# U transposed on TensorE and normalised by VectorE from PSUM, with a longer ring of exp blocks

## The chip, the cores and the metric

The kernel runs on one core of one Trainium2 chip. The metric is the device time of one execution in microseconds. TensorE (PE) multiplies matrices into PSUM, ScalarE (ACT) and VectorE (DVE) read PSUM and write SBUF, GpSimd (POOL) works from SBUF to SBUF, and SyncE (SP) issues the DMAs. The five work from instruction lists of their own and meet by semaphores.

## The reference

A layer norm of x (2048 tokens of 640) feeds two branches whose results are added to x: attention with 32 query heads of 20 columns and one shared key and value head, and a dense pair of matrices with SiLU between.

```python
x = A_x
xn = _layernorm(x, axis=-1)
return x + _A_ref(xn, A_wq, A_wk, A_wv, A_wo) + _B_ref(xn, B_w1, B_w2)
# _A_ref: q = (x @ wq) as 32 heads of 20; k = x @ wk; v = x @ wv  (20 columns each)
scores = jnp.einsum("bhqd,bkd->bhqk", q, k) * (Dh ** -0.5)
p = _softmax(scores, axis=-1)
o = jnp.einsum("bhqk,bkd->bhqd", p, v)        # heads side by side, then @ wo
# _B_ref: silu(x @ w1) @ w2, w1 640x1728, w2 1728x640
```

## The kernel before

**Units, groups and steps.** A unit is one head for one chunk of 512 queries: 32 heads by 4 chunks make 128 units. Three units form a group (43 groups, the last with two). A group runs over 16 key tiles of 128; each of these 688 steps is one score tile S (`do_S`, matmuls at L747): three matmuls, one a unit, into three PSUM banks. Banks 0 to 2 and 3 to 5 take turns, so S of step t+2 needs the banks of step t read out.

**Exponentials on two engines.** In most steps ScalarE exponentiates two of the three banks in one instruction (exp, L765) into blocks of the ring `E`, and VectorE does the third: p1 (L779) clamps the score, scaled and shifted so that its int16 bits are a bfloat16 power of two, into `Z`; once three such blocks have come together, two instructions (y, L838) make two phase-shifted copies in `Y`, and the three versions are later summed with weights built into copies of v, which evens out the error of the bit trick. Where VectorE has too much queued (`want_dve`), in the first ten steps, and in the last step of a group, ScalarE takes all three banks. E has NBLK = 31 blocks of 512 columns; an exp whose blocks don't fit before the ring's end starts again at block 0 and waits until that has been read.

**PV.** For each step and each of the Y sets, TensorE multiplies v with the blocks (L826) into PSUM bank 6 (`UBANK`), four column strips of 32 rows at once: U, 21 rows a unit, of which the last is the softmax's sum. These matmuls trail the score tiles by some steps; `pv_q` holds the ones to come, and the ring E is their store.

**End of a group** (`end_group`, `norm_dma`). VectorE copies U to SBUF (L937), and bank 6 is free for the next group. SP transposes the copy by DMA (L896), GpSimd adds up the strips in four instructions (L904, L907, L909), VectorE takes the reciprocal of the sums (L914), and GpSimd multiplies into `o` (L923). The last group alone uses another way, on TensorE and VectorE (L949, L962, L978).

**Other TensorE work,** called misc, fills the time between: q of the next chunk (L1015), h = x @ w1 (L1049; tanh on ScalarE L1057, product on VectorE L1062), and output jobs (`out_job`: 14 matmuls with w2 at L1111, 5 with wo at L1116, evicted at L1128 and L1134), all through PSUM bank 7. Each job has a step before which it may not start. What is left of it after the last S runs alone: for the last chunk's output these are eight jobs of 14 matmuls each and the short ones with wo. Matmuls of zeros (fills, L671 and L684) keep TensorE busy in gaps.

**Order.** It is made at build time by a list scheduler (`Sched`, `Builder.step`) with assumed durations. TensorE takes S when it may start, else PV or misc, not starting one that would run more than OVER past the time at which S is due. VectorE and ScalarE take the ready instruction of lowest priority number: U evacuation and reciprocal 0.9 (U_PRIO), p1 1.0, q, h and output evictions 1.6 (X_PRIO), y 4.0. `lock` keeps y and the GpSimd instructions of `norm_dma` from being planned at the same time; on the chip nothing enforces that. SP keeps plain loads in order but may pass them with q copies and transposes.

**Prologue.** x is loaded, normalised, transposed; k, v and the first q tiles are made, among them a dense q tile; the scaling of wo by 2 on GpSimd follows the k tiles. Score tiles start within the prologue; PV may start when the prologue's jobs are done or 11 PVs wait (PV_HOLD).

Of the kernel before, what the change touches and what calls it, by code (L numbers as in the profile page):

```python
# [7 lines left out]
BF16 = mybir.dt.bfloat16  # L8
F32 = mybir.dt.float32
# [5 lines left out]
P = 128  # L15
# [29 lines left out]
NUNITS = H * QC  # L45
NBLK = 31
NZ = 3
# [16 lines left out]
DT_ISSUE = 1.28  # L64
UT_ISSUE = 1.05
DT = (4, 5, 6, 7, 11, 12, 13, 14, 15)
# [9 lines left out]
class Op:  # L76
    __slots__ = ("eng", "dur", "fn", "deps", "prio", "seq", "end", "avail", "idx", "inc", "inc_no", "sem",
                 "on_sched", "name", "dma", "mode", "start", "mm", "work", "kt", "na", "rs", "re", "rl", "then", "after", "lock")

    def __init__(self, eng, dur, fn, deps, prio=0.0, name="", on_sched=None, mode=None):  # L80
        self.eng = eng
        self.dur = dur
        self.fn = fn
        self.deps = deps
        self.prio = prio
        self.name = name
        self.on_sched = on_sched
        self.mode = mode
        self.start = None
        self.end = None  # L90
# [9 lines left out]
        self.lock = False  # L100

# [5 lines left out]
class Sched:  # L107
    def __init__(self, nc, stack):
# [11 lines left out]
        self.held = {}  # L120
        self.lock_end = {"dve": 0.0, "pool": 0.0}
        self.busy = defaultdict(float)
# [42 lines left out]
    def ready(self, op, extra=0.0):  # L165
        r = 0.0
        for d in op.deps:
# [9 lines left out]
            if a > r:  # L177
                r = a
        if op.lock:
            r = max(r, self.lock_end["pool" if op.eng == "dve" else "dve"])  # L180
        return r

    def commit(self, op, start):
# [3 lines left out]
        if op.dma:  # L187
            if op.name in ("oTd", "xTd", "uTd"):
                self.dma_t = op.end
            self.dma_t = max(getattr(self, "dma_t", 0.0), op.end) + op.mode / 230e3  # L190
            op.avail = op.end + 1.6 if op.name in ("oTd", "xTd", "uTd") else max(op.end + 2.0, self.dma_t + 1.6)
        else:
            op.avail = op.end + LAT[e]
# [3 lines left out]
        self.busy[e] += op.dur  # L197
        if op.lock:
            self.lock_end[e] = op.end
        self.held[e] = op.then  # L200
# [3 lines left out]
    def run(self):  # L204
        wake = {e: 0.0 for e in self.engs}
        while True:
# [13 lines left out]
            else:  # L220
# [122 lines left out]
class Builder:  # L343
# [17 lines left out]
    def alloc(self):  # L361
# [185 lines left out]
    def step(self, now):  # L547
# [64 lines left out]
        if choice == "PV":  # L612
# [115 lines left out]
    def do_S(self, t, now):  # L728
# [78 lines left out]
        pv.kt = kt  # L807
        self.pv_last = pv
        pv.na = na
# [19 lines left out]
    def flush_z(self):  # L829
# [7 lines left out]
        for k in range(2):  # L837
            sc.new("dve", t_dve_4x(w), lambda v, k=k: v.tensor_scalar(  # L838
                self.Y[:, zs, k, 0:n * QW], Z, float(PH[k + 1][0]), None, ALU.add), zk,
                [("Y", zs, k, i) for i in range(n)], prio=4.0 + 0.1 * k, name=f"y{k}").lock = True  # L840
        ts = []
# [49 lines left out]

    def norm_dma(self, g, rows):
        sc = self.sc
        us = self.groups[g]
        up = g % 2
        op = sc.dma("sp", lambda q: q.dma_start_transpose(self.UT[:, up, :, 0:rows], self.U[0:rows, up, :]),  # L896
                    [("U", up)], [("UT", up)], rows * QW * 2, sem=self.s_UT[up], name="uTd")
        op.dur = UT_ISSUE
        self.ut_cnt[up] += 1
        op.inc_no = self.ut_cnt[up]  # L900
        ut = self.UT[:, up, :, :].rearrange("p q (i j) -> p q i j", j=SLOT)
        w = self.W
        if rows == P:
            two = lambda v: v.tensor_tensor(w[:, :, 2, :], ut[:, :, 2, 0:DH + 1], ut[:, :, 3, 0:DH + 1], ALU.add)  # L904
        else:
            two = lambda v: v.tensor_copy(w[:, :, 2, :], ut[:, :, 2, 0:DH + 1])
        pl = [(0.35, lambda v: v.tensor_copy(w[:, :, 0:2, :], ut[:, :, 0:2, 0:DH + 1])), (0.3, two)]  # L907
        for lo, hi, i in ((0, 11, 0), (11, DH + 1, 1)):
            pl.append((0.22, lambda v, lo=lo, hi=hi, i=i: v.tensor_tensor(  # L909
                w[:, :, 2, lo:hi], w[:, :, 2, lo:hi], ut[:, :, i, DH + 1:DH + 1 + hi - lo], ALU.add)))  # L910
        for n, (d, fn) in enumerate(pl):
            sc.new("pool", d, fn, [("UT", up)], [("W", n if n < 2 else 1)], prio=0.5, name=f"w{g}").lock = True
        rl = self.rL[:, up, :, :]
        sc.new("dve", 0.22, lambda v: v.reciprocal(rl, w[:, :, :, DH]), [("W", 0), ("W", 1)], [("rL", up)], prio=U_PRIO,  # L914
               name=f"rcp{g}")
        for c in sorted(set(x // H for x in us)):
            js = [j for j, x in enumerate(us) if x // H == c]
            h0, m = us[js[0]] % H, len(js)
            dst = self.o[:, c % 2, :, h0 * DH:(h0 + m) * DH].rearrange("p q (i d) -> p q i d", d=DH)
            src = w[:, :, js[0]:js[0] + m, 0:DH]  # L920
            r0 = rl[:, :, js[0]:js[0] + m]
            rb = bass.AP(self.rL, r0.offset, [list(r0.ap[0]), list(r0.ap[1]), [1, m], [0, DH]])
# [3 lines left out]
            self.norm_made[c] += m  # L926
            self.try_oT(c)

    def end_group(self, g):
# [8 lines left out]
        sc.new("dve", t_dve_ps(QW), evac, [("UB",)], [("U", up)], prio=U_PRIO, name=f"Uev{g}")  # L938

        sc.pend["dve"][-1].name = f"Uev{g}"  # L940
# [263 lines left out]
    def prologue(self):  # L1204
# [5 lines left out]
        self.out_cnt = [0] * 3  # L1210
        self.s_UT = [sem(f"UT{i}") for i in range(2)]
        self.ut_cnt = [0, 0]
        self.s_oT = [sem(f"oT{i}") for i in range(4)]
# [351 lines left out]
```

## Time and profile before

| what | value |
|---|---|
| median of three runs (least, most) | 761.34 us (760.96, 761.35) |
| the profiled execution, its span | 761.34 us, 759.5 us |
| mean granted clock of TensorE | 0.995 |
| exps of one, two, three blocks | 13, 588, 87 |
| p1 (third tiles on VectorE) | 598 of 688 |
| first score tile, first PV, last score tile | 16.6, 42.8, 730.3 us |
| DMA transposes of U; GpSimd's instructions for it | 42; 212 |

The page gives each engine's busy time and share of the span, then the span in 40 slices, the DMA queues, the chain that ended last, and the costliest groups of instructions by source line. A group's line has engine, operation, what it writes and reads, and its count; then busy time, the mean duration of one, and the engine's idle time before it with what ended it. Records of one engine overlap at their ends, so the mean duration of an instruction is longer than the distance from one start to the next. Waits are listed as: who waited, for whom, time in all, times, the longest.

### The profile page before, as it was taken

What the parts mean: (1) busy time and instruction counts of PE and PEld (TensorE: products, weight loads), DVE (VectorE), ACT (ScalarE), POOL (GpSimd) and SP (SyncE); (2) the same over time, 40 slices, a digit from 0 to 9 for tenths busy, and PEclk for the clock granted to TensorE, in tenths of its full rate; (3) what the DMA queues carried; (4) which work ended last, traced back from release to release, by engine and by line L of the source; (5) the groups of instructions that cost most, each with busy time, mean ns of one, the idle gap of its engine ahead of it and who ended that gap; (6) DMA issues with size and microseconds to landing.
All of it is one profiled execution on the core that took longest, in us unless ns stands there. A gap on an engine that the chain in (4) does not pass through costs nothing. (4 is left out here: it accounts for less than half of the span.)

```text
span 759.5 us, 17804 instructions
## 1 busy us (share of the span) xinstructions
PE 724.4 (95%) x6758; PEld 235.0 (31%) x6816; DVE 699.8 (92%) x1361; ACT 712.6 (94%) x780; POOL 107.5 (14%) x280
## 2 busy tenths in 40 slices
PE   8789999999999999999999999999999999999996
PEld 4332222222223333322223333322223333322244
DVE  7879999999999999999998999999999999999965
ACT  7879999999999999999999999999999999999930
POOL 5421111111110011111110101011000111111110
PEclk9999999999999999999999999999999999999999
DMA  6660000011020011011001110110030111000100
GB/s 185 156 215 15 14 16 15 16 22 40 25 44 25 16 39 26 15 34 22 8 17 34 33 31 14 35 33 15 9 42 8 26 27 32 26 8 8 36 9 35
DMA packets 55963, 27.06 MB, mean 36 GB/s; under 512 B 43687, under 2 KB 55239, under 8 KB 55879
## 3 DMA queue, kind: packets, MB, share of 16 engines
q1 hardware_dynamic: 54566, 25.87, 13.5%
q8 instruction: 55, 0.90, 0.5%
q10 hardware_dynamic: 1312, 0.05, 0.1%
q14 instruction: 30, 0.24, 0.1%
HBM read 11.36 MB, written 2.62 MB: 18 GB/s over the span
## 5 line engine op out<-in xcount | busy, mean ns | idle before, releaser
L765 ACT ACTIVATE sbt<-psall 128x1024 bf16<-128x1024 f32 (+1 forms) x688 | 679.7, 1131 | 14.5 <-PE psall L747 7.0
L779 DVE TENSOR_SCALAR sbt<-psall 128x512 int16<-128x512 f32 x598 | 401.1, 684 | 27.4 <-PE psall L747 22.1
L747 PE MATMUL psall<-sbt 32*128 32x512 bf16 x2048 | 269.1, 384 | 12.9 <-ACT sbt L765 6.3
L826 PE MATMUL psall<-sbt 128*32 128x512 bf16 x3413 | 265.6, 384 | 2.7 <-DVE sbt L937 1.3
L838 DVE TENSOR_SCALAR sbt<-sbt 128x1536 int16<-128x1536 int16 (+2 forms) x434 | 218.8, 527 | 2.2
L747 PEld LDWEIGHTS psall<-sbt 32*128 32x128 bf16 x2048 | 69.6, 91 | 264.6 <-ACT sbt L765 108.7
L826 PEld LDWEIGHTS psall<-sbt 128*32 128x32 bf16 x3413 | 67.0, 94 | 113.9 <-issue 73.2
L907 POOL CAST sbt<-sbt 128x168 f32<-128x168 bf16 x42 | 15.3, 364 | 547.8 <-DMA sbt<-sbt 547.8
L1111 PE MATMUL psall<-sbt 128*128 128x320 bf16 x448 | 82.5, 302 | 0.0
L1049 PE MATMUL psall<-sbt 128*128 128x512 bf16 (+1 forms) x245 | 74.9, 384 | 4.9 <-issue 3.1
L1111 PEld LDWEIGHTS psall<-sbt 128*128 128x128 bf16 x448 | 36.1, 97 | 40.2 <-issue 27.8
L1062 DVE SCALAR_TENSOR_TENSOR sbt<-sbt,psall 128x512 bf16<-128x512 bf16 (+1 forms) x56 | 38.0, 679 | 3.5 <-ACT sbt L1057 1.7
L1057 ACT ACTIVATE sbt<-psall 128x512 bf16<-128x512 f32 (+1 forms) x56 | 38.6, 690 | 0.0
L923 POOL TENSOR_TENSOR sbt<-sbt 128x240 bf16<-128x240 f32 (+2 forms) x44 | 27.7, 631 | 41.9 <-DVE sbt L914 41.5
L1049 PEld LDWEIGHTS psall<-sbt 128*128 128x128 bf16 (+1 forms) x280 | 19.7, 98 | 40.1 <-issue 23.8
L1116 PE MATMUL psall<-sbt 128*128 128x320 bf16 x160 | 30.9, 303 | 0.7 <-DVE sbt L1094 0.7
L937 DVE CAST sbt<-psall 128x512 bf16<-128x512 f32 x43 | 29.4, 683 | 1.8 <-PE psall L826 1.8
L671 PE MATMUL psall<-sbt 128*32 128x512 bf16 (+7 forms) x98 | 29.2, 363 | 0.0
L909 POOL TENSOR_TENSOR sbt<-sbt 128x44 f32<-128x44 f32 x84 | 27.8, 331 | 6.6
L684 PE MATMUL psall<-sbt 128*128 128x512 bf16 (+3 forms) x94 | 25.9, 399 | 2.8 <-POOL sbt L1261 1.4
L1015 PE MATMUL psall<-sbt 128*128 128x512 bf16 (+1 forms) x80 | 25.2, 394 | 2.2 <-issue 2.2
L1128 DVE SCALAR_TENSOR_TENSOR sbt<-psall,sbt 128x320 f32<-128x320 f32 x16 | 7.9, 492 | 10.2 <-PE psall L1111 9.7
(86 smaller groups left out, 194.1 us busy)
## 6 DMA issues: line engine op xcount, KB each, us to landing
sbt<-in_A_x_dram SPq DMA_DIRECT2D x32, 160.0 KB, 3.6
out_dram<-sbt SPq DMA_DIRECT2D x16, 160.0 KB, 1.8
sbt<-in_B_w_dram SPq DMA_DIRECT2D x5, 432.0 KB, 5.4
sbt<-sbt SPq DMA_DIRECT2D x105, 20.0 KB
sbt<-in_B_w_dram SPq DMA_DIRECT2D x13, 160.0 KB, 3.8
sbt<-sbt SPq DMA_TRANSPOSE x67, 2.5
sbt<-in_A_wo_dram SPq DMA_DIRECT2D x5, 160.0 KB, 6.0
sbt<-in_A_wq_dram SPq DMA_DIRECT2D x5, 140.0 KB, 3.8
```

Of the source, the lines that this page charges most:

```text
L671: return pe.matmul(self.bk(UBANK, 0, n, 0, 32), self.zero[:, 0:32], self.zero[:, 0:n], start=False, stop=False, tile_position=(0, 0), skip ...
L747: ins = pe.matmul(self.bk(par3 + j), self.kT[r:r + SLOT, kk, kt * P:(kt + 1) * P], self.qT[r:r + SLOT, h // 4, (x // H) % 2, :], start=Tru ...
L765: return a.activation(self.E[:, b0 * QW:(b0 + na) * QW], self.ps[:, par3 * BANK:(par3 + na) * BANK], AF.Exp, scale=ACT_SCALE)
L779: return v.tensor_scalar(self.Z[:, zs, zp * QW:(zp + 1) * QW], self.bk(bb), 0.0, ZMAX, ALU.max, ALU.min)
L826: return pe.matmul(self.bk(UBANK, 0, QW, q * SLOT, (q + 1) * SLOT), self.v[:, w, kt, :], x, start=start, stop=stop, tile_position=(0, q * ...
L838: sc.new("dve", t_dve_4x(w), lambda v, k=k: v.tensor_scalar(self.Y[:, zs, k, 0:n * QW], Z, float(PH[k + 1][0]), None, ALU.add), zk, [("Y", ...
L937: return v.tensor_copy(self.U[0:rows, up, :], self.bk(UBANK, 0, QW, 0, rows))
L1049: return pe.matmul(self.bk(b, 0, QW, 0, rows), self.w1[:, k, fk * P:fk * P + rows], self.xnT[:, k, c * QW:(c + 1) * QW], start=(k == 0), s ...
L1057: sc.new("act", t_act(QW), lambda a: a.activation(t, src, AF.Tanh, scale=0.5), [("B", b)], [("tb", tp)], prio=X_PRIO, name=f"th{c}_{fk}")
L1062: sc.new("dve", t_dve_ps(QW), lambda v: v.scalar_tensor_tensor(out=self.hT[0:rows, fk, :], in0=t, scalar=1.0, in1=src, op0=ALU.add, op1=AL ...
L1111: return pe.matmul(self.bk(b, 0, 320), self.hT[0:rows, fk, i * P:(i + 1) * P], self.w2[0:rows, fk, e0:e0 + 320], start=(m == 0), stop=(m = ...
L1116: return pe.matmul(self.bk(b, 0, 320), self.oT[:, k, i * P:(i + 1) * P], self.wo[:, k, e0:e0 + 320], start=(m == 0), stop=(m == tot - 1))
```

## The change

At the end of every group, not only the last, four matmuls of 64 columns on TensorE transpose U and add up its strips, back into bank 6 (`stk` is a 0/1 matrix for that); VectorE takes the reciprocal there and multiplies from PSUM into `o`. The DMA transpose, the GpSimd instructions, their tiles `UT` and `W` (three E blocks' worth of SBUF) and the planner's `lock` go. The next group's first PV therefore waits for the product instead of the copy. The ring E has 34 blocks instead of 31. In the planner, the pressure margin is 14 instead of 12, misc evictions have priority 0.95 instead of 1.6 (now ahead of p1), OVER is 0.2 instead of 0.1, and SP's order is strictly first in, first out. The dense q tile in the prologue, the place of the wo scaling and the three Z sets are the same in both kernels. `end_group` has no new code: its remaining part, shown above, now runs for every group.

```diff
-NBLK = 31
+NBLK = 34
-PV_PRESS = 12
+PV_PRESS = 14
-X_PRIO = 1.6
+X_PRIO = 0.95
-OVER = 0.1
+OVER = 0.2
...
-        if op.lock:
-            r = max(r, self.lock_end["pool" if op.eng == "dve" else "dve"])
...
                 if e == "sp":
-                    first = [o for o in lst if o.name in ("dma", "xTd")]
-                    lst = first[:1] + [o for o in lst if o.name not in ("dma", "xTd")] if first else lst
+                    lst = lst[:1]
...
-        self.UT = sb([P, 2, 4, P], BF16)
-        self.W = sb([P, 4, 3, DH + 1], F32)
...
-            if op.kt == KT - 1 and getattr(op, "rl", None) is not None:
-                self.u_last = [op.rl]
...
-                [("Y", zs, k, i) for i in range(n)], prio=4.0 + 0.1 * k, name=f"y{k}").lock = True
+                [("Y", zs, k, i) for i in range(n)], prio=4.0 + 0.1 * k, name=f"y{k}")
...
-    def norm_dma(self, g, rows):
-        op = sc.dma("sp", lambda q: q.dma_start_transpose(self.UT[:, up, :, 0:rows], self.U[0:rows, up, :]),
-                    [("U", up)], [("UT", up)], rows * QW * 2, sem=self.s_UT[up], name="uTd")
...
-        for n, (d, fn) in enumerate(pl):
-            sc.new("pool", d, fn, [("UT", up)], [("W", n if n < 2 else 1)], prio=0.5, name=f"w{g}").lock = True
...
-            sc.new("pool", 0.15 + 4 * m * DH * 0.00186, lambda v, dst=dst, src=src, rb=rb: v.tensor_tensor(
-                dst, src, rb, ALU.mult), [("W", 0), ("W", 1), ("rL", up)], [("o", c % 2, h0 + i) for i in range(m)],
-                prio=0.5, name=f"nrm{g}").lock = True
...
-        if g < self.NG - 1:
-            self.pv_last.rl = sc.pend["dve"][-1]
-            self.norm_dma(g, rows)
-            return
```

More of the change, by code (lines that the diff above doesn't have):

```diff
@@ L64 @@
 DT_ISSUE = 1.28
-UT_ISSUE = 1.05
 DT = (4, 5, 6, 7, 11, 12, 13, 14, 15)
@@ L77 @@
     __slots__ = ("eng", "dur", "fn", "deps", "prio", "seq", "end", "avail", "idx", "inc", "inc_no", "sem",
-                 "on_sched", "name", "dma", "mode", "start", "mm", "work", "kt", "na", "rs", "re", "rl", "then", "after", "lock")
+                 "on_sched", "name", "dma", "mode", "start", "mm", "work", "kt", "na", "rs", "re", "rl", "then", "after")
     def __init__(self, eng, dur, fn, deps, prio=0.0, name="", on_sched=None, mode=None):
@@ L99, in __init__ @@
         self.then = None
-        self.lock = False
 LAT = {"pe": 0.215, "act": 0.175, "dve": 0.14, "pool": 0.15, "sp": 0.0}
@@ L120, in __init__ @@
         self.held = {}
-        self.lock_end = {"dve": 0.0, "pool": 0.0}
         self.busy = defaultdict(float)
@@ L187, in commit @@
         if op.dma:
-            if op.name in ("oTd", "xTd", "uTd"):
+            if op.name in ("oTd", "xTd"):
                 self.dma_t = op.end
             self.dma_t = max(getattr(self, "dma_t", 0.0), op.end) + op.mode / 230e3
-            op.avail = op.end + 1.6 if op.name in ("oTd", "xTd", "uTd") else max(op.end + 2.0, self.dma_t + 1.6)
+            op.avail = op.end + 1.6 if op.name in ("oTd", "xTd") else max(op.end + 2.0, self.dma_t + 1.6)
         else:
@@ L197, in commit @@
         self.busy[e] += op.dur
-        if op.lock:
-            self.lock_end[e] = op.end
         self.held[e] = op.then
@@ L807, in do_S @@
         pv.kt = kt
-        self.pv_last = pv
         pv.na = na
@@ L890, in flush_z @@
         self.zblocks = []
-    def norm_dma(self, g, rows):
-        sc = self.sc
-        us = self.groups[g]
-        up = g % 2
-        op = sc.dma("sp", lambda q: q.dma_start_transpose(self.UT[:, up, :, 0:rows], self.U[0:rows, up, :]),
-                    [("U", up)], [("UT", up)], rows * QW * 2, sem=self.s_UT[up], name="uTd")
[L898 to L910, printed above, removed]
-        for n, (d, fn) in enumerate(pl):
-            sc.new("pool", d, fn, [("UT", up)], [("W", n if n < 2 else 1)], prio=0.5, name=f"w{g}").lock = True
[L913 to L922, printed above, removed]
-            sc.new("pool", 0.15 + 4 * m * DH * 0.00186, lambda v, dst=dst, src=src, rb=rb: v.tensor_tensor(
-                dst, src, rb, ALU.mult), [("W", 0), ("W", 1), ("rL", up)], [("o", c % 2, h0 + i) for i in range(m)],
-                prio=0.5, name=f"nrm{g}").lock = True
-            self.norm_made[c] += m
-            self.try_oT(c)
     def end_group(self, g):
@@ L938, in end_group @@
         sc.new("dve", t_dve_ps(QW), evac, [("UB",)], [("U", up)], prio=U_PRIO, name=f"Uev{g}")
-        sc.pend["dve"][-1].name = f"Uev{g}"
-        if g < self.NG - 1:
-            self.pv_last.rl = sc.pend["dve"][-1]
-            self.norm_dma(g, rows)
-            return
         def ut(pe):
@@ L1210, in prologue @@
         self.out_cnt = [0] * 3
-        self.s_UT = [sem(f"UT{i}") for i in range(2)]
-        self.ut_cnt = [0, 0]
         self.s_oT = [sem(f"oT{i}") for i in range(4)]
```

## The prediction

> **What bounds the kernel now.** I read the page's engine shares first, then the span cut at three events (the first exp that waits, the last score tile, the end), then the waits, then the order in time around those events.
>
> ```profile
> PE 724.4 (95%) x6758; PEld 235.0 (31%) x6816; DVE 699.8 (92%) x1361; ACT 712.6 (94%) x780; POOL 107.5 (14%) x280
> ```
>
> Three engines share the limit, so the stages decide. By stage (time, then each engine's busy us, then granted clock):
>
> ```profile
> 36.70:43.20 6.50, 5.24 (x62) 2.42 (x63) 3.87 (x13) 0.01 (x1) 0.48 (x1) 0.80 1.04 389
> 43.20:82.70 39.50, 36.94 (x348) 10.96 (x347) 34.65 (x64) 39.07 (x43) 7.77 (x15) 1.00 0.19 59
> 380.00:551.80 171.80, 166.56 (x1600) 52.28 (x1612) 162.37 (x303) 171.31 (x184) 19.32 (x52) 1.00 0.11 24
> 551.80:726.40 174.60, 170.04 (x1594) 52.91 (x1603) 166.73 (x313) 171.96 (x193) 21.58 (x54) 1.00 0.12 24
> 730.70:759.50 28.80, 23.09 (x170) 13.99 (x170) 13.62 (x33) 1.02 (x1) 0.00 (x0) 0.94 0.07 24
> ```
>
> From 43 to 726 us ScalarE (fourth busy column) works almost without a gap; VectorE (third) is 4 to 6% idle. Before 43 us ScalarE stands still once; after 730.7 only TensorE's chain is left. The standstill, in ScalarE's waits and in order of time:
>
> ```profile
> ACT sbt L765 <- PE psall L826: 6.5, 1, 6.5
> ...
> 29.88 6.82 ACT L765 ACTIVATE sbt<-psall 128x1536 bf16<-128x1536 f32 x5
> 43.19 8.78 ACT L765 ACTIVATE sbt<-psall 128x1024 bf16<-128x1024 f32 x9 [6.50 <-PE psall L826]
> ```
>
> Exp 10 waits for the first PV matmul (L826): ten exps have filled 30 of E's 31 blocks, exp 10 needs two, wraps to block 0, and block 0 must first be read.
>
> The end, with the one place where the old way of normalising (kept for the last group) is to be seen:
>
> ```profile
> 735.10 0.69 DVE L937 CAST sbt<-psall 128x512 bf16<-128x512 f32 x1 [1.77 <-PE psall L826]
> ...
> 735.96 0.28 PE L949 MATMUL psall<-sbt 128*128 128x64 bf16 x4
> ...
> 736.07 11.77 PE L1111 MATMUL psall<-sbt 128*128 128x320 bf16 x77
> 736.28 0.23 DVE L962 RECIPROCAL sbt<-psall 128x12 f32<-128x12 f32 x1 [0.48 <-PE psall L949]
> 736.54 0.39 DVE L978 TENSOR_TENSOR sbt<-psall,sbt 128x80 bf16<-128x80 f32 x2
> ```
>
> 77 output matmuls (L1111) stand there in one run, 11.77 / 77 = 0.153 us each: work that did not fit beside the score tiles.
>
> Durations overlap on each engine, so I use start-to-start distances of back-to-back instructions in the trace: exp of three, two, one blocks 1.331, 0.904, 0.478; tanh 0.477; p1 (L779), evacuation (L937) and h product (L1062) 0.600; y (L838) of 1536 and 1024 columns 0.465 and 0.335; an S tile or a PV group of matmuls 0.215; an h or q matmul 0.22; a change of kind on TensorE 0.1.
>
> **The change part by part.** The profiled execution took 761.34 us, which is also the median; its span is 759.5, so 1.8 lies around it. I compare the two programs' instruction lists engine by engine; up to score tile 11 (S11) they are the same on TensorE.
>
> *E ring 31 to 34.* Exp 10 and 11 fit (30 + 2 + 2 = 34), exp 12 wraps. Its release, the first PV, also moves: the list now puts it after 14 of the v matmuls (L1472) that stood ahead of it, not after 40 and four fills. On the old trace's clock I estimate their end near 40.3 and the bank free, after the q eviction, at 40.6; before, the wait ended 0.44 us after the first PV started (42.75 to 43.19). So exp 12 starts at 41.1 instead of 45.02. Gain 3.9. The v work and evictions that this pushes behind cost some back between S12 and S48: 1.0, below.
>
> *Normalising on TensorE and VectorE.* Added per group on TensorE four 64-column matmuls, 0.28 (row L949): 40 groups between S48 and S684, 11.2 us. Added on VectorE a product from PSUM of 240 columns. Rows: 80 columns 0.237; p1, 512 columns from PSUM, 0.684. Between them about 0.40, or 0.32 start to start: 40 x 0.32 = 12.8 us; the bounds are 0.24 and 0.60, so 10 to 24. The reciprocal costs 0.233 instead of 0.221. Removed: 42 DMA transposes and 212 GpSimd instructions (L904 to L923), some 86 us of an engine that nobody on the path waits for; VectorE's reciprocal waited 2.8 us for it in all. SP loses 1.23 us of issue for each transpose; nothing that S needs waits there, so that is 0, and SP's order is now strictly first in, first out, which costs nothing while DMA share stays near 0.1.
>
> *GpSimd silent.* VectorE's y runs at 469 ns start to start where no GpSimd instruction overlaps it (255 cases) and 514 where one does (52; of the narrow ones 9, by 9 ns more): 2.4 us to be saved.
>
> ```profile
> 316.84 0.55 DVE L838 TENSOR_SCALAR sbt<-sbt 128x1536 int16<-128x1536 int16 x1
> 316.85 1.02 POOL L909 TENSOR_TENSOR sbt<-sbt 128x44 f32<-128x44 f32 x2
> ```
>
> Here y keeps its usual 0.55 and GpSimd's pair, 0.66 by the row means, takes 1.02: GpSimd loses. [...]
>
> *What ScalarE does.* The share of VectorE is chosen again by the planner: 598 to 595 third tiles. Exps of two blocks 588 to 581, of three 87 to 92, of one 13 to 15: -6.3 + 6.7 + 1.0 = +1.3 us. VectorE's p1 and y lose 1.8 + 0.9.
>
> *FFN and output work.* Between S48 and the last S, TensorE's list has 47 more output matmuls and 36 fewer fills (of 0.2 each): with 11.2 for the transposes and 0.9 for q, TensorE carries 11.2 + 7.1 + 0.9 - 7.5 = +12 us there. VectorE carries 12.8 + 1.3 (evictions) - 2.4 - 2.7 + 0.5 = +9.5.
>
> *What the steady stage costs.* Lower end +1.3: ScalarE alone sets the pace and the others have room (VectorE 29.7 us idle, TensorE some 38 beyond those distances, and 20 of fills). Upper end +25: both additions (12 and 12.8) in series. To choose, I cut S48 to S684 into stretches of eight tiles, and added in each the engines' instructions times the distances above, taking the largest engine. Before: 645, where the trace has 726.4 - 82.7 = 643.7. After: 657.7. With stretches of 5, 12 or 16 the difference is 12.5, 10.3, 7.7. The reason shows in one group, S592 to S607: TensorE 14.9, ScalarE 15.3, VectorE 14.5 before; 16.1, 15.8, 15.7 after. I take +12.7, and +1.0 for new waits on TensorE, where the four matmuls wait for the evacuation and the next group's first PV for the product: today's waits on L937 are 12 us over 43 groups, nearly all covered. The same sum over S12 to S48 gives the 1.0 above.
>
> *The longer hold of PSUM bank 6* (from last PV to next group's first PV: 2.7 to 3.9 score tiles on average in the lists) I cost at nothing: exps run ahead into E, and the lead at the first PV grows from 7 to 8.1 tiles, at most 11 of the 16 that 34 blocks hold. If that cover were gone it would cost 1.2 tiles, 1.1 us, per group, 45 us. *p1 behind h, q and output evictions* (X_PRIO now below p1's 1.0): 0.6 us late against two exps of 0.9 until the bank is needed: 0; at worst 0.05 for each of 107 evictions, 5. *OVER 0.2*: TensorE may be 0.1 later on 48 more changes from misc to S: 0 to 4.8, taken 0 since the stretch sum holds that work. *PV_PRESS and NBLK* move only E's pressure point (19 to 20 blocks): 0.
>
> *The end.* Exps 684 to 687 start 4.35 us apart (726.38 to 730.73), because six output matmuls and six PV groups, 2.4 us, stand between S685 and S686. In the changed list five output matmuls stand among all four tiles; about 3 us should do: -1.3. After S687 51 L1111 matmuls are left where there were 98: 47 x 0.151 = -7.1, and two more PV groups +0.4: -6.7.
>
> Sum: -3.9 + 1.0 + 12.7 + 1.0 - 1.3 - 6.7 = +2.8, so 764.1; I say 764.
>
> **The rivals.**
> *ScalarE still sets the steady pace (faster).* Place: S48 to S684; price +1.3 to +5 instead of +13.7, since planner order lets TensorE use the 58 us of idle and fills. For it: ScalarE busy for 98.5 to 99.7% of its stages. Against it: TensorE's sums above ScalarE's in the F stretches. The ends keep -10.9, so 752 to 755.5. It decides from a steady stage longer by less than 9.4 us.
> *The chain evacuate, transpose, reciprocal, product blocks TensorE's queue (slower still).* Everything behind a waiting L949 or PV, S included, stands. The rows show 0.5 between the matmuls and the reciprocal, and up to 0.9 for a PV behind L937. 0.2 to 0.3 us at 41 groups on top of the forecast: 772 to 776.
> *It cancels.* Ends -10.9, steady +9.4 to +12.5: 760 to 763; this is the forecast with a slightly smaller steady term.
>
> **How the numbers follow.** Within 0.2% (1.5 us, 759.8 to 762.9) a measurement can't tell from no change. Forecast and its spread, 760 to 768: 0.50, of which 0.13 falls within 0.2% and 0.04 below. ScalarE-paced: 0.28, nearly all faster (0.25). Blocked queue: 0.22, slower. So faster 0.29, same 0.16, slower 0.55. The range 754 to 772 leaves out the best of the second case and the worst of the third; the forecast's own range is 760 to 768.
>
> **What the changed profile would show.** The exp that wraps starts at 41 us after a wait of 2 to 3; from last exp to end 22 us, not 28; GpSimd silent after 45 us; the product x40 at 0.40; S48 to S684 at 657. Were that stage below 653, the first rival holds; above 663, the second, and then waits of L813 or L735 on L922 or L887 would be seen, some 10 us more than today. Wrong would also be a product far from 0.40, or an end that some DMA or VectorE sets.

## The result, and the profile after

The changed kernel took 765.12 us (median; 763.85 to 765.87), the kernel before 761.15 us on the same chip (760.63 to 761.35): a ratio of 1.0052, 95% interval 1.0034 to 1.0069. It is slower by some 4 us. The profiled execution took 765.5 us, its span is 763.7. One run among those reported below, of the version a_cp, took 2942 us, which nothing in the records explains; it is left out of that version's ratio.

The engine shares of the page of the changed kernel:

```profile
PE 721.4 (94%) x6869; PEld 242.0 (32%) x6926; DVE 707.1 (93%) x1402; ACT 715.7 (94%) x780; POOL 22.8 (3%) x68
```

GpSimd's 85 us are gone, VectorE has 7 us more, and the three engines at the limit are as full as they were. Where the 4 us lie is to be seen by stage only. The span of the changed kernel, cut at the first exp that waits for the ring (exp 12, before it was exp 10), at exp 48, twice in the steady stage, and from exp 687 to the end; columns: time, busy us of TensorE, its weight loads, VectorE, ScalarE, GpSimd, then granted clock, DMA share, GB/s:

```profile
41.43:79.97 38.54, 35.58 (x375) 11.91 (x377) 35.69 (x74) 37.57 (x40) 3.72 (x5) 1.00 0.21 71
...
380.03:555.00 174.97, 168.12 (x1641) 54.69 (x1654) 165.25 (x312) 172.05 (x184) 0.00 (x0) 1.00 0.06 16
555.00:739.54 184.54, 179.20 (x1680) 59.74 (x1687) 170.68 (x328) 172.22 (x190) 0.00 (x0) 0.99 0.06 15
741.45:763.70 22.25, 16.47 (x129) 9.95 (x127) 12.75 (x31) 1.02 (x2) 0.00 (x0) 0.98 0.08 31
```

| stage, us (from exp to exp) | before | after | difference | predicted |
|---|---|---|---|---|
| span's start to exp 12 | 45.02 | 41.43 | -3.6 | -3.9 |
| exp 12 to 48 | 37.66 | 38.55 | +0.9 | +1.0 |
| exp 48 to 684 (steady) | 643.7 | 659.6 | +15.9 | +13.7 |
| exp 684 to 687 | 4.35 | 1.90 | -2.5 | -1.3 |
| exp 687 to the span's end | 28.81 | 22.25 | -6.6 | -6.7 |
| sum | 759.5 | 763.7 | +4.2 | +2.8 |

The start, from the timeline of ScalarE after the change (start, duration, instruction, idle time before it and who ended that):

```profile
38.63 1.02 ACT L753 ACTIVATE sbt<-psall 128x1024 bf16<-128x1024 f32 x1 [1.02 <-PE psall L735]
41.43 1.94 ACT L753 ACTIVATE sbt<-psall 128x1024 bf16<-128x1024 f32 x2 [1.77 <-PE psall L813]
```

The wait for the first PV matmul (now L813) is 1.77 us at exp 12, where it was 6.50 at exp 10. Exp 11 had waited 1.02 for its score tile.

In the steady stage ScalarE stands still more often than before. I took the distance of each of its instructions to the next, less its back-to-back distance from the prediction: from exp 48 to 687 these rests come to 20.3 us before and 32.9 after, while the back-to-back distances themselves went only from 627.7 to 628.6. In the waits of ScalarE after the change, what it waited for is the score tile:

```profile
ACT sbt L753 <- PE psall L735: 18.8, 26, 2.6
```

and before:

```profile
ACT sbt L765 <- PE psall L747: 7.0, 14, 2.1
```

By position in a group the increase lies in one place: over groups 3 to 40, the rests behind key tile 11 were 0.1 us and are 7.5, behind key tile 10 they were 1.0 and are 2.7; the other fourteen together went from 13.1 to 10.4. The last group adds 4.8. One such place in the order of time, around score tile 412 of the changed kernel:

```profile
447.43 1.49 DVE L825 TENSOR_SCALAR sbt<-sbt 128x1536 int16<-128x1536 int16 x3
...
448.04 1.91 PE L813 MATMUL psall<-sbt 128*32 128x512 bf16 x31
448.83 1.29 DVE L767 TENSOR_SCALAR sbt<-psall 128x512 int16<-128x512 f32 x2
449.88 0.39 PE L735 MATMUL psall<-sbt 32*128 32x512 bf16 x3
450.32 1.94 ACT L753 ACTIVATE sbt<-psall 128x1024 bf16<-128x1024 f32 x2 [0.91 <-PE psall L735]
```

TensorE's list puts eight PV groups between S411 and S412 (31 matmuls in one run). They could not start before the product had freed bank 6, at 447.52. VectorE meanwhile does three y's and takes the third bank of S410 only at 448.83; S412, which needs that bank, starts a microsecond later, and ScalarE has been without work for 0.91 us.

The product takes the time that was predicted, and TensorE waits for it (the instructions of L922, and who waited for them):

```profile
L922 DVE TENSOR_TENSOR sbt<-psall,sbt x46: 230/397/407, 56.4 to 747.2; 128x240 bf16<-128x240 f32 x40, 128x80 bf16<-128x80 f32 x4, 128x160 bf16<-128x160 f32 x2
...
  PEld psall L813: 5.1, 14
  PEld psall L735: 3.0, 6
```

**A caution for the comparisons below.** In these profiles TensorE's granted clock falls to half (0.50) in single stretches of 3.4 us, mostly at other places in another execution. In the changed kernel one lies in the steady stage:

```profile
708.40:711.80 3.40, 2.23 (x16) 0.70 (x14) 3.37 (x9) 3.40 (x6) 0.00 (x0) 0.99 0.09 18
711.80:715.20 3.40, 3.40 (x27) 1.02 (x27) 2.89 (x7) 2.75 (x4) 0.00 (x0) 0.50 0.49 98
```

Where two executions run the same order, with and without one, the stage is longer by 1.6 and 1.7 us (exp 512 to 684: 184.54 with, 182.96 without; exp 10 of the old order: 43.19 with, 41.49 without). So a difference of single profiles is known only to that, and the stages below are given with 1.6 us taken off for each such stretch ("at full clock"). Before has one at its start, after one at its start and one in the steady stage. At full clock exp 48 comes at 81.1 before and 78.4 after (-2.7), and from there to the end it is 676.9 before and 682.1 after (+5.2).

### The profile page after: what moved, and what is told of

It is laid out like the page before. It is cut to its first block, busy times and chain, and to the rows that moved or that the text cites. A ratio compares the mean times of both kernels' runs of the same rounds, so it can differ in the third digit from the quotient of the medians.

```text
span 763.7 us, 17625 instructions
## 1 busy us (share of the span) xinstructions
PE 721.4 (94%) x6869; PEld 242.0 (32%) x6926; DVE 707.1 (93%) x1402; ACT 715.7 (94%) x780; POOL 22.8 (3%) x68
## 5 line engine op out<-in xcount | busy, mean ns | idle before, releaser
L753 ACT ACTIVATE sbt<-psall 128x1024 bf16<-128x1024 f32 (+2 forms) x688 | 681.6, 1121 | 22.1 <-PE psall L735 18.8
L813 PE MATMUL psall<-sbt 128*32 128x512 bf16 x3403 | 259.8, 385 | 2.3 <-DVE sbt L922 1.0
L825 DVE TENSOR_SCALAR sbt<-sbt 128x1536 int16<-128x1536 int16 (+1 forms) x434 | 216.0, 520 | 2.0
L813 PEld LDWEIGHTS psall<-sbt 128*32 128x32 bf16 x3403 | 70.8, 95 | 113.3 <-issue 65.6
L1055 PE MATMUL psall<-sbt 128*128 128x320 bf16 x448 | 87.5, 303 | 0.4
L1055 PEld LDWEIGHTS psall<-sbt 128*128 128x128 bf16 x448 | 35.2, 97 | 43.3 <-issue 32.0
L1060 PE MATMUL psall<-sbt 128*128 128x320 bf16 x160 | 31.8, 303 | 0.7 <-DVE sbt L1038 0.7
L887 DVE CAST sbt<-psall 128x512 bf16<-128x512 f32 x43 | 29.4, 684 | 1.3 <-PE psall L813 1.1
L672 PE MATMUL psall<-sbt 128*128 128x512 bf16 (+6 forms) x85 | 23.1, 392 | 1.9 <-POOL sbt L1203 1.4
L659 PE MATMUL psall<-sbt 128*32 128x512 bf16 (+10 forms) x61 | 18.2, 352 | 0.0
L922 DVE TENSOR_TENSOR sbt<-psall,sbt 128x240 bf16<-128x240 f32 (+2 forms) x46 | 17.2, 380 | 0.1
L1060 PEld LDWEIGHTS psall<-sbt 128*128 128x128 bf16 x160 | 12.5, 97 | 14.1 <-issue 7.7
L1078 DVE SCALAR_TENSOR_TENSOR sbt<-psall,sbt 128x320 bf16<-128x320 f32 x32 | 15.0, 483 | 1.8 <-PE psall L1060 0.9
```

What stands on the lines that cost most here:

```text
L753: return a.activation(self.E[:, b0 * QW:(b0 + na) * QW], self.ps[:, par3 * BANK:(par3 + na) * BANK], AF.Exp, scale=ACT_SCALE)
L813: return pe.matmul(self.bk(UBANK, 0, QW, q * SLOT, (q + 1) * SLOT), self.v[:, w, kt, :], x, start=start, stop=stop, tile_position=(0, q * ...
L825: sc.new("dve", t_dve_4x(w), lambda v, k=k: v.tensor_scalar(self.Y[:, zs, k, 0:n * QW], Z, float(PH[k + 1][0]), None, ALU.add), zk, [("Y", ...
L887: return v.tensor_copy(self.U[0:rows, up, :], self.bk(UBANK, 0, QW, 0, rows))
L1055: return pe.matmul(self.bk(b, 0, 320), self.hT[0:rows, fk, i * P:(i + 1) * P], self.w2[0:rows, fk, e0:e0 + 320], start=(m == 0), stop=(m = ...
L1060: return pe.matmul(self.bk(b, 0, 320), self.oT[:, k, i * P:(i + 1) * P], self.wo[:, k, e0:e0 + 320], start=(m == 0), stop=(m == tot - 1))
```

## The experiments

Ratios are to the kernel before on the same chip, with the 95% interval; on the chips of the later versions its median was 760.4 to 760.9 us. "Exp 48 to the end" is from the profile, at full clock.

| run | ratio | median, us | exp 48 | exp 48 to the end |
|---|---|---|---|---|
| before | 1 | 761.15 | 81.1 | 676.9 |
| after | 1.0052 (1.0034 to 1.0069) | 765.12 | 78.4 | 682.1 |
| b_hold10 | 1.0016 (1.0008 to 1.0025) | 761.39 | 79.4 | 679.4 |
| a_n31 | 1.0087 (1.0069 to 1.0106) | 767.01 | 81.5 | 682.1 |
| a_nb25 | 1.0099 (1.0083 to 1.0114) | 767.38 | 81.9 | 681.5 |
| b_dve | 1.0029 (1.0018 to 1.0040) | 762.49 | 81.1 | 679.8 |
| b_pe | 1.0097 (1.0082 to 1.0111) | 767.53 | 82.0 | 683.3 |
| a_ut1 | 1.0056 (1.0043 to 1.0070) | 764.97 | 77.6 | 681.9 |
| a_cp | 1.0023 (1.0015 to 1.0032) | 762.77 | 78.2 | 681.9 |
| b_up | 1.0022 (1.0013 to 1.0031) | 762.09 | 80.5 | 679.2 |
| a_nz4 | 1.0089 (1.0075 to 1.0103) | 767.20 | 81.2 | 681.9 |
| b_consts | 1.0047 (1.0035 to 1.0059) | 764.33 | 80.3 | 680.9 |
| a_consts | 1.0244 (1.0226 to 1.0262) | 779.64 | 77.6 | 691.9 |
| a_x | 1.0248 (1.0224 to 1.0272) | 778.47 | 76.7 | 692.1 |

### The start: the ring

The old kernel with PV allowed one step earlier, b_hold10:

```diff
-PV_HOLD = 11
+PV_HOLD = 10
```

> The kernel before with one number changed: PV may start once 10 PVs wait (PV_HOLD 10, not 11), so that the wrapped exp 10 no longer stands until the prologue is over. The rest of TensorE's order is that of before but for a few tiles. If the ring's standstill is worth what the forecast said (3.9 us at exp 12, 1.0 given back up to S48), exp 10 starts near 39.5 instead of 43.2 us and the time falls by 3 to 4 us, to 757 to 758.5. If the standstill is made up later anyway (the rival: the prologue's v work is only pushed behind and ScalarE waits for it there), the time stays within 1 us of before, 760 to 762.

Exp 12 started at 39.41 us, 5.6 earlier than in the profile of before, and exp 12 to 48 then took 41.58 us instead of 37.66. At full clock 1.7 us of the gain were left at exp 48 (79.4 instead of 81.1); the rest of the execution, whose list is planned anew, took 2.5 us longer, and the whole is 0.16% slower. So an earlier first PV was no gain in the end; most of it went by exp 48, where the prologue's work that had stood ahead of it had still to be done.

The changed kernel with the old ring, a_n31, and with a ring smaller still but the same order from S64 on, a_nb25:

```diff
-NBLK = 34
+NBLK = 31
```

> The changed kernel with the ring of 31 blocks. The planner orders anew; its list leaves 101 output matmuls behind the last S (before 98, changed kernel 51). My theory: the ring saves some 3.3 us at the start, and output work moved from the end into the steady stage is a wash, because TensorE is the limit in both. Then this is the changed kernel plus 3 to 4 us, 768 to 769.5: steady stage +5 to +8 against before (normalising alone), end and start as before. Rival, that the output matmuls moved into the steady stage cost less there than they save at the end: the loss of 50 matmuls' room (7 us) shows in full, 771 to 773. Rival, that the ring does nothing: 764 to 766.

```diff
-NBLK = 34
-PV_PRESS = 14
+NBLK = 25
+PV_PRESS = 5
```

> The changed kernel with a ring of 25 blocks and PV_PRESS 5 (the same pressure point, 20 blocks); from S48 on its order is that of the changed kernel, so it shows the ring's worth at the start alone and stands beside a_nz4. Exp 8 instead of exp 12 wraps. Theory: 2 to 4 us slower than the changed kernel, all of it before S48, ratio 1.008 to 1.010. Rival, that the standstill is made up in the prologue (as in b_hold10): ratio 1.005 to 1.006.

a_nb25 came as expected, a_n31 1 us below its range. Exp 48 comes at 81.5 and 81.9 instead of 78.4, and the rest is the same within 0.6 us: the longer ring is worth about 3 us, all of it at the start. a_n31 tells one thing more. Its list leaves 101 L1055 matmuls behind the last score tile, not 51; its end is 30.10 us long (7.9 more), its steady stage 651.1 (8.5 less). The output work that the change moved from the end into the steady stage is therefore neither gain nor loss.

### Is it the added time on TensorE or on VectorE?

Time added to the old kernel, in its old order. b_dve, some 0.27 us of VectorE (0.29 in the trace) after each reciprocal, 11 to 12 us in all:

```diff
-        sc.new("dve", 0.22, lambda v: v.reciprocal(rl, w[:, :, :, DH]), ...
+        def rcp(v):
+            v.reciprocal(rl, w[:, :, :, DH])
+            f = w.rearrange("p a b c -> p (a b c)")[:, 0:192]
+            return v.tensor_tensor(self.st6[:, :, :, :].rearrange("p a b c -> p (a b c)"), f, f, ALU.add)
+        sc.new("dve", 0.22, rcp, ...
```

> The kernel before in the very order of before, with one instruction more on VectorE behind each of the 42 reciprocals (a sum of 192 float columns into a dead tile, about 0.27 us, 11 us in all), off every chain. It prices VectorE's load alone, without the chain through bank 6. Theory, by the sum over stretches of eight tiles: +3.2 us, 764 to 765, since VectorE has 4.6% idle and only some stretches are its own. Rival, that VectorE's load is what the change costs: +8 to +11. Rival, that ScalarE alone sets the pace: +0 to +1.

b_pe, 0.28 us of TensorE in each group, zeros added into bank 6 at key tile 8, 12 us in all:

```diff
+            if kt == 8:
+                for n in (QW, 160):
+                    ins = pe.matmul(self.bk(UBANK, 0, n, 0, SLOT), self.v[:, 0, kt, :], self.zero[:, 0:n], start=False,
+                                    stop=False, tile_position=(0, 0), skip_group_check=True)
```

> The kernel before in the very order of before, with 0.28 us more on TensorE in every group (zeros added to U in the step of key tile 8, 512 and 160 columns; the result stays the same), 12 us in all, off every chain. It prices TensorE's load alone. Theory, by the sum over stretches of eight tiles: +2.8 us, 763.5 to 764.7. Rival, that TensorE is the limit of the whole steady stage: +9 to +12. Rival, that ScalarE alone sets the pace: +0 to +1.

VectorE's 11 us cost 2.1 us, less than the 3.2 expected; TensorE's 12 us cost 7.2, more than the 2.8 expected. Where the order does not know of it, TensorE's time is the dearer one: about 60% of it is paid.

Time taken away from the changed kernel, in its order. a_ut1 issues only one of the four transposing matmuls. From the first of them to the next matmul behind them it is 0.127 us in the changed kernel and 0.039 in a_ut1 (medians of 43 groups), so this takes 3.8 us off TensorE in all, not the 8.4 of the expectation:

```diff
-            for qt in range(4):
+            for qt in range(1):
...
+        xv = bass.AP(self.ps, xv.offset, [list(xv.ap[0]), [0, 4], list(xv.ap[2]), list(xv.ap[3])])
```

> The changed kernel in its very order, but of the four 64-column matmuls that transpose U only the first is issued, and reciprocal and product read its result four times (three quarters of every query tile's output are left out and stand in for by the first quarter's). It takes about 0.2 us off TensorE in each group, 8.4 us in all, and leaves VectorE and the number of waits as they are. Where 12 us more on TensorE cost the kernel before 7 us (b_pe), 8.4 us less should give 5 back: ratio to before near 1.000. Rival, that the wait chain through bank 6 and not TensorE's load costs the time: less than 2 us back, ratio 1.003 or more.

a_cp replaces the product from PSUM by a copy from SBUF, 0.129 us from start to start instead of 0.312, 7.3 us in all:

```diff
-                ... lambda v, dst=dst, src=src, rb=rb: v.tensor_tensor(
-                    dst, src, rb, ALU.mult), [("UB",), ("rL", up)], ...
+                ... lambda v, dst=dst, m=m: v.tensor_copy(
+                    dst, self.U[:, up, 0:4 * m * DH].rearrange("p (q i d) -> p q i d", q=4, d=DH)),
+                    [("UB",), ("rL", up), ("U", up)], ...
```

> The changed kernel in its very order, with the product from PSUM replaced by a copy of as many columns from the evacuated U in SBUF (the normalisation is left out). About 0.18 us less on VectorE in each group, 7.6 in all, and the next group's first PV is released that much sooner. By the rate that b_dve showed (2 us for 11) this gives 1.5 back, ratio to before 1.003 to 1.004. Rival, that VectorE's chain at the group's end holds TensorE's queue: 4 us or more back, ratio 1.000 or less.

Neither gives the loss back. The steady stage of a_ut1, with two half-clock stretches in it, is no shorter than that of the changed kernel with one (659.57):

```profile
79.17:740.19 661.02, 641.42 (x6050) 200.06 (x6042) 624.70 (x1184) 642.85 (x690) 0.00 (x0) 0.99 0.06 16
```

At full clock exp 48 to the end is 681.9 in both, against 682.1 (changed kernel) and 681.5 (a_nb25, which has its order and no such stretch). Exp by exp the three executions run together: counted from exp 48, the changed kernel is never more than 0.4 us behind a_cp up to exp 656, and a_ut1 is behind by that and the 1.5 us of its stretch at 168.4. a_cp's median is 2.3 us lower all the same; its profile has no half-clock stretch before the very end, where that of the changed kernel has two, and the mean clock of its runs is 0.995 to 0.999, against 0.992 to 0.996. So with the order as it is, 3.8 us of TensorE or 7.3 us of VectorE are worth nothing. By elimination the loss lies in the order: in what waits for what. What the two versions leave in (one matmul, the copy, the reciprocal) is not tried, nor both at once; but b_consts, below, shows that a new order without any added work can lose as much.

### The hold of bank 6, and what is full first

b_up makes the old kernel hold bank 6 longer, by moving the copy of U and the reciprocal back in VectorE's order: 3.7 score tiles between last and first PV in the list, where before has 2.7 and after 3.9. No work is added; but the list is planned anew, and 16 output matmuls move from the end into the steady stage.

```diff
-U_PRIO = 0.9
+U_PRIO = 4.5
```

> The kernel before with one planner number changed: U_PRIO 4.5 instead of 0.9, so VectorE copies U out of bank 6 only when nothing else is ready. No work is added; bank 6 is held longer, 3.7 score tiles between a group's last PV and the next one's first (before 2.7, changed kernel 4.0), and 82 output matmuls are left behind the last S instead of 98. New theory: it is the hold of bank 6 that costs, since Z has room for nine VectorE blocks only, some ten tiles, and p1 must wait for PVs that stand behind the bank. Then the steady stage S48 to S684 grows by 4 to 7 us, of which 2.4 come back at the end: 763 to 766, ratio 1.003 to 1.006. Rival, that the added work costs and the hold is covered by the ring E: 759 to 761.5, ratio 0.998 to 1.001.

1.7 us slower, between the two expectations; and ScalarE's rests grow behind key tile 10 (5.7 us, before 1.0) as they do behind 11 in the changed kernel. The hold is not free, though the prediction had taken it so; some cover ends.

Which one, a_nz4 tells: the changed kernel with four Z sets instead of three, 12 blocks of VectorE's results, and the small ring.

```diff
-NBLK = 34
-NZ = 3
-PV_PRESS = 14
+NBLK = 25
+NZ = 4
+PV_PRESS = 5
```

> As a_nb25, with four Z and Y sets instead of three (their SBUF comes from the ring): room for twelve VectorE blocks while PVs wait for bank 6. New theory: ScalarE's waits at key tiles 10 and 11, 10 us in the changed kernel, shrink to 3 or less, and S48 to S684 gets 8 to 11 us shorter than in a_nb25. Its list leaves 111 output matmuls behind the last S instead of 51, 9 us: so the time is a_nb25's within 2 us, TensorE's work being only moved to the end. Rival, that E or the load and not Z makes these waits: they stay, and the steady stage shortens by no more than the output work that left it, evenly over the key tiles.

The rests behind key tile 11 fall from 6.4 us (a_nb25) to 1.0, with the same ring of 25 blocks, so E is not what made them. Behind key tile 10 they do not fall (2.8 and 3.4), so that the two together miss the 3 that was expected; three waits of an exp for a PV, 2.2 us, stand there, in which the small ring E was full. In the last group the rests fall from 10.3 to 4.4. The steady stages of a_nb25 and of a_nz4:

```profile
83.51:740.87 657.36, 631.60 (x6128) 203.26 (x6169) 624.00 (x1184) 641.58 (x690) 0.00 (x0) 1.00 0.06 16
```

```profile
84.43:731.20 646.77, 620.03 (x6052) 197.41 (x6093) 617.78 (x1171) 640.74 (x688) 0.00 (x0) 1.00 0.06 16
```

and the place of the timeline above, in a_nz4:

```profile
447.80 5.18 ACT L753 ACTIVATE sbt<-psall 128x1536 bf16<-128x1536 f32 x5
...
450.23 0.40 PE L813 MATMUL psall<-sbt 128*32 128x512 bf16 x4
...
450.89 0.40 PE L813 MATMUL psall<-sbt 128*32 128x512 bf16 x4
451.11 1.28 DVE L767 TENSOR_SCALAR sbt<-psall 128x512 int16<-128x512 f32 x2
```

There the PV groups go one at a time between the score tiles, and ScalarE does not stop. So it was Z, with nine blocks for some ten steps, that was full while the PVs were held: VectorE could take no third bank until a PV had read a block. The changed kernel's list shows it at the place above: p1 of S410 writes the block of Z that the PV of tile 400 reads, and that PV is the first of the run behind S411. On the chip p1 waited for a PV six times in the changed kernel,

```profile
DVE sbt L767 <- PE psall L813: 3.9, 6, 0.9
```

four times in a_nb25 (2.5 us), three times in the old kernel (0.8 us), and never in a_nz4. Not all that the steady stage wins is Z's, though: 60 output matmuls have left it, some 9 us of TensorE, and a_n31, with 101 left over and three Z sets, has 3.8 us behind key tile 11. And yet the time did not move. The list leaves 111 output matmuls behind the last tile instead of 51, the end is 31.27 us instead of 22.23, and exp 48 to the end is 681.9 against 681.5. The wait behind key tile 11 is real and its cause is shown, but taking it away gives nothing by itself here: what the steady stage wins, the planner spends on its own output work at the end.

### The planner's numbers

The three numbers that the change sets anew, in the old kernel (b_consts), and the old ones in the changed kernel (a_consts); then only the priority of the evictions put back (a_x):

```diff
-PV_PRESS = 12
-X_PRIO = 1.6
-OVER = 0.1
+PV_PRESS = 14
+X_PRIO = 0.95
+OVER = 0.2
```

> The kernel before with the changed kernel's planner numbers alone (X_PRIO 0.95, OVER 0.2, PV_PRESS 14), its DMA transposes, GpSimd work and ring of 31 kept. The sums over its new order give -1 us, 97 output matmuls are left behind the last S as before: 759 to 762, ratio 0.998 to 1.002. Rival, that these numbers (evictions ahead of p1, TensorE allowed later) are what makes the changed kernel slower: ratio 1.004 or more.

```diff
-PV_PRESS = 14
-X_PRIO = 0.95
-OVER = 0.2
+PV_PRESS = 12
+X_PRIO = 1.6
+OVER = 0.1
```

> The changed kernel with the planner numbers of before (X_PRIO 1.6, OVER 0.1, PV_PRESS 12): normalising on TensorE and VectorE and the ring of 34 alone. Theory, that the normalising work costs the time whatever the numbers: 763 to 767, ratio 1.003 to 1.008, though its list leaves only 40 output matmuls behind the last S (-8.8 us there, paid in the steady stage). Rival, that the numbers cost the time: ratio 0.996 to 1.000.

```diff
-X_PRIO = 0.95
+X_PRIO = 1.6
```

> The changed kernel with one planner number put back: X_PRIO 1.6 in place of 0.95, so that the evictions of q, h and output jobs are again planned behind p1 (the prediction costed that order at nothing, at worst 5 us). The planner now leaves 112 of the L1055 output matmuls behind the last score tile, where the changed kernel leaves 51; in the run with 31 blocks and in the run with four Z sets that alone was made up by a shorter steady stage. Theory: the priority by itself costs next to nothing either way, and the 14.5 us lost with all three old numbers come from their working together: ratio to before 1.004 to 1.008, the end some 31 us long, S48 to S684 some 8 to 10 us shorter than in the changed kernel. Rival: the priority is the number that the changed layout needs, since the product and the reciprocal then stand beside p1 without room for the evictions: most of the 14.5 us come back as a loss, ratio 1.016 to 1.025, S48 to S684 of 665 us or more.

The first two missed: each kernel loses by the other's numbers, the old one 3.4 us, the changed one 14.5. b_consts came out at its rival's ratio. Without any added work the new numbers cost the old kernel 4.0 us behind exp 48 at full clock (680.9 against 676.9), where the whole change costs 5.2; and in its list no group from 3 to 40 has ten tiles of lead at the first PV, and p1 waited for a PV once (0.3 us), so that this loss is not the wait for Z. But a_consts shows that the changed kernel does not get it back with the old numbers. The third missed too, and is the largest effect of all runs. X_PRIO alone costs 13 us in the changed kernel (778.47 against 765.12), as much as the three together (ratios 1.0248 and 1.0244). At full clock it loses 10.0 behind exp 48 (692.1 against 682.1, with all three 691.9) and wins 1.7 ahead of it; the remaining 5 us of the medians go with a lower mean clock (0.985 to 0.989 in its runs, 0.992 to 0.996 in those of the changed kernel). The rival that I had put beside it came true, but for its steady stage of 665 us (661.7). Its steady stage and its end:

```profile
78.30:739.97 661.67, 635.82 (x6107) 199.45 (x6107) 621.48 (x1175) 642.51 (x688) 0.00 (x0) 0.99 0.06 16
742.33:775.20 32.87, 26.74 (x193) 15.73 (x190) 15.86 (x37) 1.62 (x3) 0.00 (x0) 0.94 0.06 21
```

It has about the output work behind the last tile that a_nz4 has (112 matmuls), but not a_nz4's short steady stage. ScalarE rests 34.2 us between exp 48 and 687, where a_nz4 has 20.8; up to 4.8 of the difference are put down to the clock (three half-clock stretches at 1.6), and 12.5 us of the rests in groups 3 to 40 lie behind key tile 11 (1.0 in a_nz4). There one sees the wait for Z at first hand:

```profile
450.91 0.55 DVE L825 TENSOR_SCALAR sbt<-sbt 128x1536 int16<-128x1536 int16 x1
...
451.41 1.48 PE L813 MATMUL psall<-sbt 128*32 128x512 bf16 x24
451.86 2.74 DVE L767 TENSOR_SCALAR sbt<-psall 128x512 int16<-128x512 f32 x4 [0.40 <-PE psall L813]
...
453.26 1.94 ACT L753 ACTIVATE sbt<-psall 128x1024 bf16<-128x1024 f32 x2 [0.71 <-PE psall L735]
```

VectorE has nothing it may do until the PV run has started (0.40 us, ended by L813), then takes four third banks in a row, and ScalarE has stood 0.71 us for its score tile. Why the later evictions lead there more often is not settled; only that they do, and that it takes this number alone.

## Why the prediction was right, and where it was not

The forecast was 764.0, slower; measured were 765.12 and a ratio of 1.0052. The sum over the stages was +2.8; at full clock the profile gives -2.7 + 5.2 = +2.5. In the two profiled executions the rest, 1.6, is the one half-clock stretch that the changed kernel has more. For the medians that is an inference: the changed kernel's runs have a mean granted clock of 0.992 to 0.996, the runs of before 0.994 to 1.000 with most at 0.996 or above, and among the changed kernel's own runs the span goes from 762.0 at 0.996 to 764.1 at 0.992; but among the runs of before time and clock hardly go together (at 0.999 their times are 759.2 to 761.1 us, at 0.995 759.9 to 761.4), and the mean also counts the half clock behind the last matmul (in the profile of before the last 3.5 us of the span, where the last matmul ends at 754.5).

- **Ring at the start (-3.9, +1.0): held.** Exp 12 at 41.43 (41.1 forecast), after a wait of 1.77; -2.7 up to exp 48 at full clock. a_n31 and a_nb25 confirm that it is the ring; b_hold10, with the earlier PV alone, kept 1.7 of its gain up to exp 48 and lost it behind.
- **The end (-1.3 and -6.7): held together.** -2.5 and -6.6; the first is nearly twice its forecast.
- **GpSimd silent (-2.4): the size held, tried in no run of its own.** The y's of 1536 columns went from a mean of 561 ns to 551 (328 of them, -3.3 us), those of 1024 from 422 to 431 (100, +0.9). "GpSimd loses" holds for the pair shown, where y had started first. In the profile of before, the 28 y's of 1536 columns that started while a GpSimd instruction ran took 0.55 to 0.95 us, 21 of them 0.60 or more and three, beside L923, 0.95; the 35 beside which one started later took 0.50 to 0.56.
- **The product at 0.40: held,** 0.397. Of TensorE's waits on L922 and L887 together there are 18.6 us, where L937 had 12.2 before: +6.4, more than the +1.0 of the sum and less than the 10 that would have meant the rival of the blocked queue.
- **The steady stage (+13.7): right in size, wrong in its reason.** 657.0 was promised; the trace has 659.6 with one half-clock stretch, and 657.4 in a_nb25 with the same order and none. But I had made it of TensorE's 11.2 us and VectorE's 12.8. The 11.2 were mis-read: 0.28 is the length of L949's row, while the next matmul starts 0.11 behind its start in the rows shown, and 0.127 in the changed kernel, so the transposes take some 5 us. a_ut1 took 3.8 us of them away, and a_cp 7.3 of VectorE's, and nothing came back, where at b_pe's rate the 3.8 alone should have given 2.3. That the size came out all the same is in part luck: the same sum over stretches gave -1 for b_consts (measured +3.4), +2.8 for b_pe (7.2) and +3.2 for b_dve (2.1), and for this change +7.7 to +12.7 by the length of the stretches. About half of the term is output work that has only moved there from the end (47 matmuls, 7.1 us); the other half is the order with its waits. No run separates that half further: ScalarE's own instructions account for 0.9 of it, and what the waits at key tiles 10 and 11 cost could not be won alone.
- **The step that failed: "X_PRIO ... 0; at worst 5".** I priced the new priority by what it delays (p1 behind an eviction) and found room for that. What it does for the changed layout I did not ask. a_x measured it: without it the changed kernel loses 13 us more, 8.3 of them at full clock. The sum was not spoiled, since it was made over the lists that the number had already shaped; but the working gives no hint that the list stands on it. OVER and PV_PRESS, also put at 0, add nothing measurable to it (a_consts against a_x).
- **The other failed step: "the longer hold of PSUM bank 6 I cost at nothing".** I named the ring E as its cover and counted 8.1 of 16 tiles. The cover that ends first is Z, nine blocks or some ten steps, which I had not counted; in 16 of the 38 groups 3 to 40 the lead at the first PV reaches ten (in one before). b_up, with one more tile of hold, no work added and its list planned anew, measured +1.7 us. It is far from the 45 us that I had named for a hold without cover.
- **A row of before, mis-read:** from 43 to 83 us VectorE is 12% idle (busy 34.65 of 39.50 us), not 4 to 6%; the sum does not use it.
- **The rivals.** ScalarE as the sole pace (752 to 755.5) needed less than 9.4 us more in the steady stage: it got 15.9, and ScalarE rests more than before, not less. The blocked queue needed 663 us or more there: 659.6. That the parts cancel (760 to 763) was the nearest, and misses by 2 us, about what the clock took.

No version among these runs is faster than the kernel before.

## What to carry to other kernels

When a scheduler's numbers change together with the code, price each number in the new layout too: here one priority was worth 8 us at full clock and 13 as measured, while the operations that the change is about, made cheaper one at a time, were worth nothing. What an operation took from its engine here was the distance to the next instruction's start and not the length of its row: 0.127 us for the four transposing matmuls, whose row (L949, before) has 0.28. When a release gets later, list every buffer that fills up meanwhile and take the shortest; the largest one, which is the one in mind, was not the limit. Where the engines are all 95% full, compare stages and not sums of busy time, and move the same amount of left-over work to the same side before saying which order is better.

## What the runs showed of the hardware that I had not expected

In these profiles the clock that TensorE is granted drops to half (0.50) for one stretch of 3.4 us at a time, and not at the same places in two executions, even of one order: in the changed kernel at 35.9 and 711.8 us; in a_ut1 at 28.5, 168.4 and 711.2; in a_cp not before the very end. In a_x it is at 27.4, 167.4, 467.7 and 635.0; in before at 35.9; in b_dve and b_pe not before the very end. Where it was measured, one was worth 1.5 to 1.7 us.

In the 3.40 us directly ahead of a stretch TensorE was busy for 2.47 us in before (73%, ahead of 35.9), and for 2.56 and 2.23 us in the changed kernel (75 and 66%, ahead of 35.9 and 711.8), against some 95% of the whole span. Shares of 66% (2.25 of 3.40 us, from 462.6 in the changed kernel) and of 76% (2.58, from 706.8 in a_cp) were followed by the full clock. What brings a stretch on, these runs do not show.

Time added to TensorE outside the order cost 60% of itself (7.2 us for 12 in b_pe), time taken from it within the order gave back nothing (3.8 us in a_ut1). The two are not opposites, and one can't be read from the other.
